# Attention scores from stacked rounded halves on the whole array, in a fused attention and two expert layers kernel

## The chip, the cores and the metric

One core of a Trainium2 chip. The metric is the device time of one execution in microseconds; the median of three runs is compared.

## The reference

```python
scores = scale * np.matmul(q, k.transpose(0, 1, 3, 2))     # B, H, S, D = 4, 8, 576, 64; fp32
scores = np.where(causal, -1e9, scores); a = softmax(scores)
local = np.matmul(a, v)
mem_out = einsum(phi(q), M_prev) / (einsum(phi(q), z_prev) + 1e-6)
x = g * mem_out + (1 - g) * local                          # g = sigmoid(beta), by head
h = x @ w_in;  x = (h * sigmoid(h)) @ w_out                # 2304 x 512 -> 2048 -> 512
g = x @ w_gate; out = (g * sigmoid(g) * (x @ w_val)) @ w_out   # 512 -> 1536 -> 512
```

The weights are float64; the rest is fp32.

## The kernel before, in words

Attention works on pairs of heads: the two 64-deep heads of a pair lie on partitions 0 to 63 and 64 to 127. The 576 query rows fall into blocks of 128 (blocks 0 to 3) and a last one of 64, and into two parts: the first 256 rows, and the other 320. There are three phases. Phase A is the first part of batch 0 (four pairs), phase B the second part of batch 0 (four pairs), phase F all rows of batches 1 to 3 (twelve pairs).

For a pair, `transposed` brings q and k into columns by TensorE (PE) transposes, and ScalarE (ACT) moves them out of PSUM as `Q` and `K` (in A and B `K` is the kept tile `kT`). `pa` makes phi(q). `s_blk(i)` computes the scores of block i, `w = 128 (i + 1)` keys wide, for both heads (line 394): a fp32 matmul of 64 rows each, with the query block as the stationary operand and the keys moving. VectorE (DVE) adds the mask and takes the row minimum (line 399; the sign of the scale is turned), ACT takes the exponential (line 403). `s_blk4` does the last 64 rows of both heads in one matmul on 128 rows. `norm` inverts the sums and GpSimd (POOL) scales the rows (line 436). `T_A` and `T_B` transpose the weights on PE, `AV` multiplies with v, and `put_x` splits the result into two rounded parts, `xh` and `xl`.

The two expert layers take every matrix product as three matmuls of fp32r, a rounded form of fp32: rounded by rounded, remainder by rounded, rounded by remainder. `s1` in `moe1` is the first product of the first layer (line 757, tile `h`), followed by tanh on ACT, a product on DVE (line 765), the rounding on ACT (`gh`) and the remainder on POOL (`gl`); line 801 is the second product (tile `y`). Lines 894 and 922 are those of the second layer. Weights are decoded from float64 by three DVE instructions (`decode`, lines 627 to 629) between a step on ACT and the rounding, and kept in DRAM as `wd` for later batches.

The order is made in two steps. The strings `opA`, `opB` and `opF` list a pair's steps, and each `+` ahead of a name moves it one slot on; the next pair begins 1, 7 or 8 slots later. `attn_slot` writes out one slot's steps; the loop at the end calls it at a rate set by the goals of the expert work of the first layer. Then the framework's scheduler reorders what was written by the times that it estimates; each engine executes its list in order. `att` gives the attention tiles their buffers: 4 in A, 2 in B, 2 in F.

Of the kernel before, what the change touches and what calls it, by code (L numbers as in the profile page):

```python
# [9 lines left out]
F32R = mybir.dt.float32r  # L10
# [7 lines left out]
P = 128  # L18
# [10 lines left out]
    T2=384,  # L29
# [22 lines left out]
    n0=8,  # L52
# [8 lines left out]
    ey=0,  # L61
    yr=['yx', 'y3'],
    n_rows=2,
    n_s4=dict(A=0, B=2, F=2),
    lb=3,
    bufsA={'*': 4},
    bufsB={'*': 2},
    bufsF={'*': 2},
    stepA=1,
    stepB=7,  # L70
    stepF=8,
    opA='q0 k0 ++pa s0 s1 ++m0 n0 ++TA ++V0',
    opB='q1 k1 ++pa lq ++s2 ++s3 ++m1 lb s4 ++++n1 +++T0 +T1 +T2 +T3 +T4 ++V1 lv',
    opF='q0 k0 +q1 k1 ++pa lq +s0 s1 ++s2 ++n0 s3 ++s4 m0 +m1 lb ++TA ++V0 n1 ++++T0 +T1 +T2 +T3 +T4 ++V1 lv',
    qev='a',
    kev='a',
    q4='p',
# [8 lines left out]
def kernel(  # L86
# [15 lines left out]
    nc = tc.nc  # L102
    B, H, S, D = q.shape
# [15 lines left out]
    def f(ap):  # L119
        return ap.bitcast(F32)  # L120
# [47 lines left out]
    cur = {}  # L168

    def att(shape, tag, bufs=1, dt=F32):  # L170
        return cur["pool"].tile(shape, dt, tag=tag, name=tag, bufs=cur["bufs"].get(tag, cur["bufs"].get("*", bufs)))

    def open_at(name):
        if "x" in cur:
# [13 lines left out]
    def cp(e, out, in_):  # L188
        if e == "a":
            nc.scalar.copy(out, in_)  # L190
        else:
            (nc.vector if e == "v" else nc.gpsimd).tensor_copy(out, in_)
# [7 lines left out]
    def tt(e):  # L200
        return nc.vector if e == "v" else nc.gpsimd
# [21 lines left out]
    def bd_of(u):  # L223
        b, p, _ = units[u]
        return bds[b % 2][:, p]
# [70 lines left out]
    def unit(u):  # L296
        b, p, sups = units[u]
        o = {}
        ph = "A" if sups == (0,) else "B" if sups == (1,) else "F"
        co = 0 if 0 in sups else SA  # L300
# [28 lines left out]
        def qT(sup):  # L329
            if "Q" not in o:  # L330
                o["Q"] = att([P, W], "Q", 2)
            d = slice(0, SA) if sup == 0 else slice(SA - co, S - co)
            transposed("q", sup, o["Q"][:, d], E("qev"), 1.0)
            if sup == 1:
                o["q4"] = q4s[u % 2]
                for hh in range(2):
                    r = slice(64 * hh, 64 * hh + 64)
                    cp(E("q4"), o["q4"][r, r], o["Q"][r, 512 - co:S - co])

        def kT(sup):  # L340
            if ph == "F":
                if "K" not in o:
                    o["K"] = att([P, S], "K", 2)
            else:
                if p not in keep:
                    keep[p] = kp.tile([P, S], F32, name=f"kT{p}")
                o["K"] = keep[p]
            d = slice(0, SA) if sup == 0 else slice(SA, S)
            transposed("k", sup, o["K"][:, d], E("kev"), QSCALE)

        def pa():
            e = att([P, W], "e", 2)
            qp = att([P, W], "qp", 2)
            nc.vector.tensor_scalar_min(e, o["Q"], 0.0)
            nc.scalar.activation(out=e, in_=e, func=ACTF.Exp)
            nc.vector.scalar_tensor_tensor(qp, o["Q"], 0.0, e, ALU.max, ALU.add)
            o["qp"] = qp

        def mm(sup):

            ps = ps_a.tile([P, 512], F32, tag="a", name="psm")
            for i, c in enumerate(BLK[sup]):
                x = P * c - co if c < 4 else S - P - co
                nc.tensor.matmul(ps[:, 130 * i:130 * i + 130], o["qp"][:, x:x + P], bd_of(u), start=True, stop=True)  # L364
            nb = len(BLK[sup])
            pv = ps[:, 0:130 * nb].rearrange("p (c n) -> p c n", c=nb)
            n = att([P, nb, 2], f"n{sup}", 2)
            nc.vector.tensor_scalar_add(n, pv[:, :, 128:130], 1.0e-6)
            nc.vector.reciprocal(n, n)
            nc.vector.tensor_mul(n, n, g_bc[:, hs2].unsqueeze(1).to_broadcast([P, nb, 2]))  # L370
            if sup == 1:
                nc.vector.memset(n[0:64, 2], 0.0)
            mr = att([P, nb, 2, D], f"mr{sup}", 2)
            nc.vector.tensor_mul(
                mr, pv[:, :, 0:128].rearrange("p c (h d) -> p c h d", h=2),
                n.unsqueeze(3).to_broadcast([P, nb, 2, D]),
            )
            o["mr", sup] = mr

        def new_small(sup):  # L380
            if ("mn", sup) in o:
                return
            o["mn", sup] = att([P, 8], f"mn{sup}", 2)
            o["sm", sup] = att([P, 8], f"sm{sup}", 2)

        def s_blk(i):
            sup = 0 if i < 2 else 1
            new_small(sup)
            w = P * (i + 1)
            pss = [ps_a.tile([P, 512], F32, tag="a", name="pss") for _ in range(2)]  # L390
            for hh in range(2):
                r = slice(64 * hh, 64 * hh + 64)
                x = P * i - co
                nc.tensor.matmul(pss[hh][:, :w], o["Q"][r, x:x + P], o["K"][r, 0:w], start=True, stop=True)  # L394
            for hh in range(2):
                col = (i % 2) * 2 + hh
                a = att([P, w], f"s{hh}{i}", 1)
                mn = o["mn", sup][:, col:col + 1]
                nc.vector.tensor_tensor_reduce(  # L399
                    out=a, in0=pss[hh][:, :w], in1=mask[:, 512 - w:512], op0=ALU.add, op1=ALU.min,  # L400
                    scale=1.0, scalar=3.0e38, accum_out=mn,
                )
                nc.scalar.activation(  # L403
                    out=a, in_=a, func=ACTF.Exp, scale=-1.0, bias=mn, accum_out=o["sm", sup][:, col:col + 1]
                )
                o["a", hh, i] = a
# [131 lines left out]
        def nxt_bd():  # L538
            if ph != "A" and p == NP - 1 and b + 2 < B:
                load_bd(b + 2, nc.sync)  # L540

        ops = {
            "q0": (qT, 0), "q1": (qT, 1), "k0": (kT, 0), "k1": (kT, 1), "pa": (pa,), "m0": (mm, 0), "m1": (mm, 1),
            "lq": (nxt_load, "qk"), "lv": (nxt_load, "v"), "lb": (nxt_bd,), "n0": (norm, 0), "n1": (norm, 1),
            "s4": (s_blk4,), "TA": (T_A,), "V0": (AV, 0), "V1": (AV, 1),
        }
# [2 lines left out]
        for i in range(4):  # L549
            ops["s%d" % i] = (s_blk, i)  # L550
# [3 lines left out]
        for nm in names:  # L554
            for d in DEPS.get(nm, "").split():
                assert d not in at_ or at_[d] < at_[nm], (d, nm)
# [12 lines left out]
        return CFG["step" + ph], [run(st) for st in stages]  # L569

    DEPS = dict(
        pa="q0 q1", s0="q0 k0", s1="q0 k0", s2="q1 k0 k1", s3="q1 k0 k1", s4="q1 k0 k1", lq="q0 q1 k0 k1",
        m0="pa", m1="pa", lb="m0 m1", n0="s0 s1", n1="s2 s3 s4", TA="n0", V0="TA m0", V1="T4 m1", lv="V0 V1",
        T0="n1", T1="T0", T2="T1", T3="T2", T4="T3",
# [5 lines left out]
    for u, key in enumerate(units):  # L580
        step, stages = unit(u)
        if u == NP:
            stages.insert(0, lambda: open_at("atB"))
            at_slot = max(slots) + 1
        if u == 2 * NP:
            stages.insert(0, open_F)
            at_slot = max(slots) + 1
        for i, st in enumerate(stages):
            slots.setdefault(at_slot + i, []).append(st)
        for sup in key[2]:  # L590
            ready[key[0], sup] = at_slot + len(stages)
        at_slot += step
# [235 lines left out]
    T2 = CFG["T2"]  # L828
# [103 lines left out]
    if True:  # L932
# [8 lines left out]
        for sg in segs:  # L941
            r = ready[sg["b"], sg["blk"][0] // SA]
# [5 lines left out]
        for kind, val in items:  # L948
# [7 lines left out]
            else:  # L956
                cost += val
                while goals and goals[0][0] <= cost:
                    c0, s0 = goals.pop(0)
                if goals:  # L960
                    x = (cost - c0) / (goals[0][0] - c0)
# [60 lines left out]
```

## Time and profile before

| | before |
|---|---|
| three runs, us | 1153.06, 1154.47, 1152.6 |
| median, us | 1153.06 |
| profiled execution: own time / span, us | 1154.19 / 1152.4 |
| granted TensorE clock, mean | 0.988 |
| busy: PE, DVE, ACT, POOL, us | 1120.4, 538.3, 440.4, 432.1 |
| DMA | 126.01 MB, mean 109 GB/s |

The span is that of the engines' instructions; the execution's own time holds 1.8 us more. A PE record's end is modelled and overlaps the next record, so what a matmul costs in a row of others is read from the distance of two starts.

### The profile page before, as it was taken

What the parts mean: (1) busy time and instruction counts of PE and PEld (TensorE: products, weight loads), DVE (VectorE), ACT (ScalarE), POOL (GpSimd) and SP (SyncE); (2) the same over time, 40 slices, a digit from 0 to 9 for tenths busy, and PEclk for the clock granted to TensorE, in tenths of its full rate; (3) what the DMA queues carried; (4) which work ended last, traced back from release to release, by engine and by line L of the source; (5) the groups of instructions that cost most, each with busy time, mean ns of one, the idle gap of its engine ahead of it and who ended that gap; (6) DMA issues with size and microseconds to landing.
All of it is one profiled execution on the core that took longest, in us unless ns stands there. A gap on an engine that the chain in (4) does not pass through costs nothing.

```text
span 1152.4 us, 18609 instructions
## 1 busy us (share of the span) xinstructions
PE 1120.4 (97%) x7016; PEld 1000.2 (87%) x7016; DVE 538.3 (47%) x1321; ACT 440.4 (38%) x1072; POOL 432.1 (37%) x480
## 2 busy tenths in 40 slices
PE   6899999999999999999989999989999999999998
PEld 4576877789989889989888999879999999999997
DVE  6996777785345442254397237852121211211211
ACT  6754766663443443343354214432121121211211
POOL 4575575564323323233275235552131311311311
PEclk8989999999999999999999999999999999999999
DMA  9975755462434413433178533420010000100000
GB/s 230 284 216 168 238 176 169 152 183 73 132 122 144 144 35 107 131 120 121 53 236 274 179 104 98 147 82 28 1 55 1 22 34 1 47 10 1 28 1 28
DMA packets 126634, 126.01 MB, mean 109 GB/s; under 512 B 72528, under 2 KB 108368, under 8 KB 126544
## 3 DMA queue, kind: packets, MB, share of 16 engines
q1 hardware_dynamic: 124368, 124.42, 34.7%
q8 instruction: 55, 0.90, 0.3%
q10 hardware_dynamic: 2176, 0.40, 0.2%
q14 instruction: 35, 0.29, 0.1%
HBM read 98.58 MB, written 26.21 MB: 108 GB/s over the span
## 4 chain that ended last, share of the span: by engine, by line
PE 82%; DVE 9%; ACT 3%; POOL 2%; issue 2%; DMA 1%; ACTq 0%; SPq 0%; POOLq 0%; DVEq 0%
PE g L894 23%; PE y L801 16%; PE h L757 16%; PE po L922 11%; PE pss L394 5%; PE U L527 4%; PE pst L317 3%; DVE raw L628 3%; DVE raw L629 2%; DVE raw L627 1%; PE psm L364 1%; ACT raw L626 1%; PE pss L422 1%; POOL wlo L669 1%; PE psq L317 1%
## 5 line engine op out<-in xcount | busy, mean ns | idle before, releaser
L767 POOL TENSOR_TENSOR gl<-th,gh 128x256 fp32r<-128x256 f32 (+1 forms) x128 | 108.6, 851 | 214.2 <-ACT gh L190 106.8
L909 POOL TENSOR_TENSOR pl<-sg,ph 128x384 fp32r<-128x384 f32 x71 | 74.3, 1046 | 300.6 <-ACT ph L907 300.6
L757 PE MATMUL h<-xh,w 128*128 128x320 f32 (+1 forms) x1024 | 170.3, 304 | 3.5 <-ACT w L190 1.2
L801 PE MATMUL y<-gh,w 128*128 128x320 f32 (+1 forms) x1024 | 167.7, 303 | 4.4 <-DVE th L765 4.4
L903 DVE SCALAR_TENSOR_TENSOR sg<-sg,g 128x384 f32<-128x384 f32 x72 | 39.7, 553 | 257.8 <-ACT sg L902 257.8
L757 PEld LDWEIGHTS h<-xh,w 128*128 128x128 f32 x1024 | 144.5, 190 | 18.0 <-issue 7.9
L801 PEld LDWEIGHTS y<-gh,w 128*128 128x128 f32 x1024 | 144.2, 190 | 17.5 <-issue 6.2
L436 POOL TENSOR_TENSOR s<-s,r 128x128 f32<-128x128 f32 (+4 forms) x144 | 115.3, 833 | 79.0 <-DVE r L453 41.1
L902 ACT ACTIVATE sg<-g 128x384 f32<-128x384 f32 x72 | 35.3, 491 | 190.2 <-PE g L894 190.2
L765 DVE SCALAR_TENSOR_TENSOR th<-th,h 128x256 f32<-128x256 f32 (+1 forms) x128 | 57.3, 449 | 98.5 <-ACT th L764 98.3
L894 PE MATMUL g<-yh,wlo 128*128 128x384 f32 x456 | 99.3, 337 | 1.5 <-POOL wlo L669 1.5
L894 PE MATMUL g<-yh,whi 128*128 128x384 f32 x456 | 98.8, 337 | 1.1 <-ACT whi L190 0.9
L894 PE MATMUL g<-yl,whi 128*128 128x384 f32 x456 | 99.4, 337 | 0.0
L801 PE MATMUL y<-gl,w 128*128 128x320 f32 (+1 forms) x512 | 92.9, 300 | 0.7 <-POOL gl L767 0.5
L757 PE MATMUL h<-xl,w 128*128 128x320 f32 (+1 forms) x512 | 92.9, 300 | 0.0
L190 ACT CAST gh<-th 128x256 fp32r<-128x256 f32 (+1 forms) x128 | 55.4, 432 | 93.7 <-DVE th L765 47.5
L907 ACT CAST ph<-sg 128x384 fp32r<-128x384 f32 x72 | 36.9, 513 | 138.1 <-DVE sg L904 138.0
L403 ACT ACTIVATE s<-s,mn 128x128 f32<-128x128 f32 (+3 forms) x128 | 71.3, 558 | 45.6 <-DVE mn L399 44.6
L894 PEld LDWEIGHTS g<-yh,whi 128*128 128x128 f32 x456 | 81.7, 188 | 7.0 <-ACT whi L190 1.3
L894 PEld LDWEIGHTS g<-yh,wlo 128*128 128x128 f32 x456 | 81.2, 188 | 1.9 <-POOL wlo L669 1.8
L894 PEld LDWEIGHTS g<-yl,whi 128*128 128x128 f32 x456 | 81.5, 189 | 0.0
L757 PEld LDWEIGHTS h<-xl,w 128*128 128x128 f32 x512 | 76.4, 191 | 4.5 <-issue 4.0
(110 smaller groups left out, 1950.5 us busy)
## 6 DMA issues: line engine op xcount, KB each, us to landing
w<-wd SPq DMA_DIRECT2D x80, 512.0 KB, 3.9
wd<-w SPq DMA_DIRECT2D x32, 512.0 KB, 4.0
raw<-in_moe_w_out_dram SPq DMA_DIRECT2D x28, 512.0 KB, 4.1
raw<-in_moe_w_in_dram SPq DMA_DIRECT2D x16, 512.0 KB, 5.0
raw<-in_moe_w_gate_dram SPq DMA_DIRECT2D x12, 512.0 KB, 3.6
raw<-in_moe_w_val_dram SPq DMA_DIRECT2D x12, 512.0 KB, 3.7
y<-yd SPq DMA_DIRECT2D x24, 192.0 KB, 2.5
out_dram<-ot SPq DMA_DIRECT2D x18, 256.0 KB, 2.1
```

The source lines that it names most:

```text
L190: nc.scalar.copy(out, in_)
L317: nc.tensor.matmul(dst, src, ident[0:n, 0:n], start=start, stop=True, is_transpose=True, skip_group_check=True)
L394: nc.tensor.matmul(pss[hh][:, :w], o["Q"][r, x:x + P], o["K"][r, 0:w], start=True, stop=True)
L403: nc.scalar.activation(out=a, in_=a, func=ACTF.Exp, scale=-1.0, bias=mn, accum_out=o["sm", sup][:, col:col + 1])
L436: nc.gpsimd.tensor_mul(a, a, r.to_broadcast([P, w]))
L757: nc.tensor.matmul(ps[:, :nt], w[:, kk, :], x[:, kk, :nt], start=(m == 0), stop=(m == 3 * KD - 1))
L765: nc.vector.scalar_tensor_tensor(th[:, :nt], th[:, :nt], 1.0, ps[:, :nt], ALU.add, ALU.mult)
L767: tt(CFG["gl" if n >= CFG["n0"] else "gl0"]).tensor_sub(gl[:, :nt], th[:, :nt], f(gh[:, :nt]))
L801: nc.tensor.matmul(ps[:, :nt], w[:, c], g[:, :nt], start=(m == 0), stop=(m == last))
L894: nc.tensor.matmul(ps[:, :T2], w[:, kk, :], y[kk], start=(m == 0), stop=(m == 3 * KD - 1))
L909: tt("v" if end else CFG["pl"]).tensor_sub(pl, sg, f(ph))
L922: nc.tensor.matmul(po[t], a[:, c], w, start=(j == 0 and n == 0), stop=(j == F2 - 1 and n == 2))
```

## The change

For blocks 0 to 3 in phase F and blocks 2 and 3 in phase B, a new step `st` (`stack`) builds three tiles in SBUF. `S` holds, for each head, the rounded q on the head's own 64 partitions and the remainder of q on the other 64. `Kh` holds the rounded k of the head on both halves, `Kl` the remainder of k on both halves. A block's scores are then two fp32r matmuls on all 128 rows that add up in PSUM: `S` against `Kh` and `S` against `Kl`. The roundings and copies are ACT's (two of q, four of k), one subtraction for each half of `S` and one half of `Kl` are DVE's, the other half of `Kl` POOL's. Phase A and the last 64 rows keep the old form.

The attention tiles of F get one buffer instead of two (also one `s4` tile); tiles of up to 8 columns get two in every phase, where A had four. The lists `opB` and `opF` are written anew: the last stage of a pair in F is 15 slots behind its first (25 before), in B 23 (21 before), and `lb`, the loads of M and z for the batch after the next, moves to the pair's end.

```diff
-    n_s4=dict(A=0, B=2, F=2),
+    n_s4=dict(A=0, B=2, F=1),
...
-    bufsF={'*': 2},
+    bufsF={'*': 1},
...
-    opB='q1 k1 ++pa lq ++s2 ++s3 ++m1 lb s4 ++++n1 +++T0 +T1 +T2 +T3 +T4 ++V1 lv',
-    opF='q0 k0 +q1 k1 ++pa lq +s0 s1 ++s2 ++n0 s3 ++s4 m0 +m1 lb ++TA ++V0 n1 ++++T0 +T1 +T2 +T3 +T4 ++V1 lv',
+    opB='q1 k1 ++pa lq st ++++s2 ++s3 ++m1 s4 ++++n1 +++T0 +T1 +T2 +T3 +T4 ++V1 lv lb',
+    opF='q0 k0 +q1 k1 ++pa lq st ++s0 s1 +s2 +s3 n0 +m0 m1 s4 +TA n1 +V0 ++T0 T1 +T2 T3 +T4 +V1 lv lb',
+    qh='a',
+    kh='aaaa',
+    kl='p',
...
     def att(shape, tag, bufs=1, dt=F32):
-        return cur["pool"].tile(shape, dt, tag=tag, name=tag, bufs=cur["bufs"].get(tag, cur["bufs"].get("*", bufs)))
+        return cur["pool"].tile(shape, dt, tag=tag, name=tag, bufs=cur["bufs"].get(tag, 2 if shape[-1] <= 8 else cur["bufs"].get("*", bufs)))
...
+        def stack():
+
+            nqs = 512 - co
+            S2 = att([P, 2, nqs], "S", 1, F32R)
+            KH, KL = (att([P, 2, 512], "K" + x, 1, F32R) for x in "hl")
+            Q, K = o["Q"][:, 0:nqs], o["K"][:, 0:512]
+            own_ = [slice(64 * hh, 64 * hh + 64) for hh in range(2)]
+            for hh in range(2):
+                r, x = own_[hh], own_[1 - hh]
+                cp(E("qh"), S2[r, hh], Q[r])
+                cp(E("kh")[hh], KH[r, hh], K[r])
+                nc.vector.tensor_sub(S2[x, hh], Q[r], f(S2[r, hh]))
+                cp(E("kh")[2 + hh], KH[x, hh], K[r])
+                tt(E("kl")).tensor_sub(KL[r, hh], K[r], f(KH[r, hh]))
+                nc.vector.tensor_sub(KL[x, hh], K[r], f(KH[r, hh]))
+            o["S"], o["KH"], o["KL"] = S2, KH, KL
...
+            x = P * i - co
             for hh in range(2):
-                r = slice(64 * hh, 64 * hh + 64)
-                x = P * i - co
-                nc.tensor.matmul(pss[hh][:, :w], o["Q"][r, x:x + P], o["K"][r, 0:w], start=True, stop=True)
+                if "S" in o:
+                    for n, part in enumerate(("KH", "KL")):
+                        nc.tensor.matmul(
+                            pss[hh][:, :w], o["S"][:, hh, x:x + P], o[part][:, hh, 0:w], start=(n == 0), stop=(n == 1)
+                        )
+                else:
+                    r = slice(64 * hh, 64 * hh + 64)
+                    nc.tensor.matmul(pss[hh][:, :w], o["Q"][r, x:x + P], o["K"][r, 0:w], start=True, stop=True)
```

Three places in the engines' lists. PE, third pair of batch 1, blocks 2 and 3 (`pss` are the scores, `h` and `y` the expert layer's two products, `pst` the transposes of the softmax rows, `U` the products with v), before:

```order
L394 MATMUL pss<-K,Q 128x384
L801 MATMUL y<-gl,w 128x320 x3
L394 MATMUL pss<-K,Q 128x384
L801 MATMUL y<-gh,w 128x320
L317 MATMUL pst<-ident,s_1449 128x128 x4
...
L394 MATMUL pss<-K,Q 128x512
L801 MATMUL y<-gh,w 128x320 x2
L394 MATMUL pss<-K,Q 128x512
```

and in the changed kernel:

```order
L415 MATMUL pss<-Kh,S 128x384
L415 MATMUL pss<-Kl,S 128x384
L828 MATMUL y<-gh,w 128x256 x3
L828 MATMUL y<-gl,w 128x256 x2
L415 MATMUL pss<-Kh,S 128x384
L415 MATMUL pss<-Kl,S 128x384
...
L415 MATMUL pss<-Kh,S 128x512
L415 MATMUL pss<-Kl,S 128x512
L415 MATMUL pss<-Kh,S 128x512
L415 MATMUL pss<-Kl,S 128x512
```

Before, the heads of a block stand apart, with expert matmuls between them; now each head's two matmuls follow each other, and whether the heads stand apart changes nothing in the rows used.

DVE, the first pair of phase B, before (`raw` is a weight being decoded):

```order
L628 SCALAR_TENSOR_TENSOR raw<-raw_317,raw 128x512
L354 TENSOR_SCALAR e<-Q 128x320
L629 SCALAR_TENSOR_TENSOR raw<-raw_317,raw 128x512
L356 SCALAR_TENSOR_TENSOR qp<-Q,e 128x320
L627 TENSOR_SCALAR raw<-raw 128x512
L628 SCALAR_TENSOR_TENSOR raw<-raw_373,raw 128x512
```

and in the changed kernel:

```order
L655 SCALAR_TENSOR_TENSOR raw<-raw_317,raw 128x512
L357 TENSOR_SCALAR e<-Q 128x320
L376 TENSOR_TENSOR Kl<-kT_157,Kh 64x512
L656 SCALAR_TENSOR_TENSOR raw<-raw_317,raw 128x512
L376 TENSOR_TENSOR Kl<-kT_157,Kh 64x512
L373 TENSOR_TENSOR S<-Q,S 64x256 x2
L359 SCALAR_TENSOR_TENSOR qp<-Q,e 128x320
L654 TENSOR_SCALAR raw<-raw 128x512
```

The four subtractions stand between the steps that decode the weights. ACT, the same pair in the changed kernel, where the four `Kh` and two `S` casts are new:

```order
L199 ACTIVATE Q<-psq 128x320
L193 CAST Kh<-kT_157 64x512 x4
L193 CAST S<-Q 64x256 x2
L358 ACTIVATE e<-e 128x320
L653 ACTIVATE raw<-raw_373 128x512
L193 CAST w<-raw 128x512
L791 ACTIVATE th<-h 128x256 x2
```

The six casts stand ahead of a weight's rounding and of the expert layer's first tanh.

## Rows read from the trace of the kernel before

**Rows 1.** Busy time of each engine by stretch.
```profile
core 0: us, PE busy (x) PEld busy (x) DVE busy (x) ACT busy (x) POOL busy (x), PEclk, DMA share, GB/s
119.00:546.00 427.00, 427.00 (x3036) 370.64 (x3035) 233.41 (x713) 210.83 (x565) 180.70 (x229) 1.00 0.44 137
30.00:119.00 89.00, 81.73 (x519) 61.25 (x520) 71.97 (x178) 51.63 (x128) 52.86 (x55) 0.92 0.72 218
```
**Rows 2.** The chain of waits from 119 to 546 us: shares by line.
```profile
by line: PE h L757 32.3%; PE y L801 31.6%; PE pss L394 11.1%; PE U L527 7.4%; PE pst L317 7.1%; PE psm L364 3.1%; PE pss L422 2.8%; PE psq L317 1.9%; PE psk L317 1.4%; PE U L317 1.3%
```
**Rows 3.** The chain of waits from 30 to 119 us (the answer ends there).
```profile
by line: PE h L757 8.6%; DVE raw L628 8.2%; issue 7.9%; PE y L801 7.7%; DVE raw L629 7.4%; PE U L527 7.3%; POOL s L436 7.2%; DVE s L399 5.4%; PE pss L394 4.3%; PE pst L317 3.6%; DVE tb L192 3.4%; ACT raw L626 3.4%; DVE raw L627 2.9%; DVE s 
```
**Rows 4.** Timeline of PE, lone heads: start, us, engine, line, operation, count.
```profile
83.75 0.28 PE L757 MATMUL h<-xl,w 128*128 128x256 f32 x1
83.97 0.91 PE L394 MATMUL pss<-kT,Q 64*128 64x384 f32 x2
84.80 0.63 PE L757 MATMUL h<-xl,w 128*128 128x256 f32 x3
85.27 0.99 PE L757 MATMUL h<-xh,w 128*128 128x256 f32 x7
...
133.88 0.48 PE L394 MATMUL pss<-K,Q 64*128 64x128 f32 x2
134.29 1.44 PE L801 MATMUL y<-gh,w 128*128 128x320 f32 x8
...
143.85 0.91 PE L394 MATMUL pss<-K,Q 64*128 64x384 f32 x2
144.69 1.14 PE L757 MATMUL h<-xh,w 128*128 128x320 f32 x6
...
146.71 1.12 PE L394 MATMUL pss<-K,Q 64*128 64x512 f32 x2
147.76 0.86 PE L527 MATMUL U<-ta,v_t 128*64 128x256 f32 x6
```
**Rows 5.** Timeline of PE, both heads next to each other.
```profile
329.08 0.92 PE L394 MATMUL pss<-K,Q 64*128 64x384 f32 x4
329.92 1.21 PE L801 MATMUL y<-gh,w 128*128 128x256 f32 x8
```
**Rows 6.** Timeline of PE, expert matmuls of 256, 384 and 512 columns.
```profile
663.79 0.64 PE L757 MATMUL h<-xl,w 128*128 128x256 f32 x4
664.27 1.12 PE L757 MATMUL h<-xh,w 128*128 128x256 f32 x8
...
796.75 0.86 PE L894 MATMUL g<-yl,whi 128*128 128x384 f32 x4
797.45 0.39 PE L922 MATMUL po<-whi,ph 128*128 128x512 f32 x1
797.68 0.39 PE L922 MATMUL po<-wlo,ph 128*128 128x512 f32 x1
```
**Rows 7.** ACT groups, 119 to 546 and 30 to 119 us: count, busy us, mean ns.
```profile
L190 ACT CAST w<-raw 128x512 fp32r<-128x512 f32 x16 | 9.8, 614 | 3.5 <-PE y L801 1.7 <-DVE raw L629 1.6
...
L190 ACT CAST gh<-th 128x256 fp32r<-128x256 f32 x8 | 3.2, 405 | 5.4 <-DVE th L765 5.4
```
**Rows 8.** A POOL group, 119 to 546 us.
```profile
L669 POOL TENSOR_TENSOR w<-raw,w 128x512 fp32r<-128x512 f32 x16 | 22.2, 1388 | 15.0 <-ACT w L190 12.8 <-issue 2.2
```
**Rows 9.** DVE line 628: min/median/max; groups of 119 to 546, 30 to 119 us.
```profile
L628 DVE SCALAR_TENSOR_TENSOR raw<-raw,raw x68: 674/693/1814, 15.0 to 764.4; 128x512 int32<-128x512 int32 x68
...
L628 DVE SCALAR_TENSOR_TENSOR raw<-raw,raw 128x512 int32<-128x512 int32 x16 | 12.7, 796 | 0.1
...
L628 DVE SCALAR_TENSOR_TENSOR raw<-raw,raw 128x512 int32<-128x512 int32 x14 | 14.3, 1024 | 0.2
```
**Rows 10.** A DVE group from 30 to 119 us.
```profile
L292 DVE TENSOR_TENSOR xl<-U,xh 128x256 fp32r<-128x256 f32 x3 | 1.2, 410 | 0.0
```
**Rows 11.** An ACT group of the whole span: the exponentials of block 3.
```profile
L403 ACT ACTIVATE s<-s,mn 128x512 f32<-128x512 f32 x32 | 23.0, 720 | 14.1 <-DVE mn L399 13.9
```

More of the change, by code (lines that the diff above doesn't have):

```diff
@@ L542, in unit @@
         ops = {
-            "q0": (qT, 0), "q1": (qT, 1), "k0": (kT, 0), "k1": (kT, 1), "pa": (pa,), "m0": (mm, 0), "m1": (mm, 1),
+            "q0": (qT, 0), "q1": (qT, 1), "k0": (kT, 0), "k1": (kT, 1), "pa": (pa,), "st": (stack,), "m0": (mm, 0), "m1": (mm, 1),
             "lq": (nxt_load, "qk"), "lv": (nxt_load, "v"), "lb": (nxt_bd,), "n0": (norm, 0), "n1": (norm, 1),
@@ L571 @@
     DEPS = dict(
+        st="q0 q1 k0 k1",
         pa="q0 q1", s0="q0 k0", s1="q0 k0", s2="q1 k0 k1", s3="q1 k0 k1", s4="q1 k0 k1", lq="q0 q1 k0 k1",
```

## The prediction

> **What bounds the kernel now.** I read first the busy times of the engines by stretch, since an average over the program hides the stages, then the chain of waits of each stretch, and last the timeline of the engine that the chain names [rows 1 to 4]. From 119 to 546 us, where pairs of heads of batches 1 to 3 are interleaved with the first expert layer, TensorE (PE) is busy for all of its 427.00 us [rows 1] and the chain of that stretch [rows 2] holds nothing but PE lines: there a microsecond less on PE is a microsecond less in the end, as long as nothing else comes last. From 30 to 119 us (second query blocks of batch 0, weights decoded for the first time) PE is busy for 81.73 of 89 us at a granted clock of 0.92, VectorE (DVE) for 71.97, and the chain [rows 3] changes hands: its visible PE lines (not all are printed) sum to 31.5%, DVE to 27.3%, POOL to 7.2%, ACT to 3.4%, "issue" to 7.9%. Behind 546 us come no scores; the change can only shift that part.
>
> Line 394, the scores that the change rewrites, is 11.1% of the first chain, 0.111 x 427 = 47.4 us, and 4.3% of the second, 3.8 us.
>
> **What a score block costs on PE now.** The timeline shows each head's matmul as two records, on 64 of the 128 rows. A 384-wide block of one head, with expert matmuls before and after it, takes PE from 83.97 to 84.80, 0.83 us, and another one 0.84 from 143.85; a 512-wide one takes 1.05, a 128-wide one 0.41 [rows 4]. Where both heads stand next to each other (four records) the two 384-wide ones together also take 0.84 us, from 329.08 to 329.92 [rows 5]: they run side by side. So what counts is the number of stretches, not of matmuls. Around each there is a toll: the one 256-wide matmul at 83.75 holds PE for 0.22 us instead of 0.12, and three behind the scores take 0.47 instead of 0.36 [rows 4, 6], together 0.20. I count 60 stretches between 119 and 526 us: 60 x 0.20 = 12 us, which the chain books to the neighbours. Sum for batches 1 to 3: 47.4 + 12 = 59.4 us.
>
> The Trainium skill (TensorEngine Tiling (Array Packing), section Theoretical Speedup) promises up to 2x from two row tiles where the contraction is 64 deep, which speaks against giving the tiles up. The trace agrees for adjacent heads [rows 5]; a lone head gets nothing of it [rows 4]. By the rule alone the old scores would cost 42 us instead of 59.4 (rival 4).
>
> **What takes its place.** Each head's block becomes two one-pass matmuls over all 128 rows (stacked q against the rounded k, then against its remainder). Rows 6 price that kind by the distance of starts: 256 wide 0.48/4 = 0.12 us, 384 wide 0.70/4 = 0.175, 512 wide 0.23. A 128-wide one is not in the trace: below it cannot cost nothing, above stands the pass of a lone 128-wide score, 0.41/2 = 0.205 [rows 4]; I take 0.12, the row of the same kind next to it. A pair: 4 x (0.12 + 0.12 + 0.175 + 0.23) = 2.58 us; twelve pairs 30.9 us, and no toll, since the neighbours use the whole array too. **Gain on PE: 59.4 - 30.9 = 28.5 us**, with 0.205 for the narrow blocks 24.4.
>
> **The stack step** is new in 16 pairs: six casts on ACT, four subtractions on DVE, two on POOL, 64 partitions each. A cast of 512 costs 0.61 us, of 256 0.41 [rows 7]; a subtraction on POOL 1.39 [rows 8]. On DVE a 512-long operation with two SBUF inputs takes 0.674 at the least and 1.814 at the most, on average 0.80 in the long stretch and 1.02 in the early one [rows 9]. That spread on one shape is a wait inside the instruction. The Trainium skill (GPSIMD Engine Reference, Key points) says that GpSimd shares its SBUF interfaces with VectorE and contends with DVE instructions that have two SBUF inputs, as all four subtractions have; the trace agrees in the spread. At the undisturbed median of 0.69 the step would cost a late pair 2.8 us of DVE, at the mean 3.2; I take the mean.
>
> From 119 us on that is 12 x 4 x 0.80 = 38 us more on DVE (233 to 271 of 398.5 us, 68%), 12 x 6 x 0.61 = 44 on ACT (211 to 255, 64%), 12 x 2 x 1.39 = 33 on POOL (181 to 214, 54%) [rows 1]. Idle time there hides it; without that cover, every microsecond that the step holds up an expert matmul comes back. In the order, the stack inputs stand several microseconds of expert matmuls ahead of their use. I charge 2 us in all for new waits.
>
> **Batch 0's second blocks, 30 to 119 us.** PE: by the order 11 stretches become 32 one-pass matmuls, 6 x 0.84 + 5 x 1.05 + 9 x 0.2 (where blocks follow each other the toll is paid once) = 12.1 us against 16 x (0.175 + 0.23) = 6.5, a gain of 5.6 if all of it ended last. DVE: 4 x (2 x 0.41 + 2 x 1.02) = 11 us more [rows 9, 10], ACT 4 x (4 x 0.61 + 2 x 0.41) = 13, POOL 8 x 1.39 = 11, the last two ahead of the weight splits that PE waits for. I scale each by its engine's visible share of the chain divided by 0.773, which the visible lines sum to: DVE 11 x 0.35 = 3.9, POOL 11 x 0.09 = 1.0, ACT 13 x 0.04 = 0.5, PE -5.6 x 0.41 = -2.3. **Net +3 us.** Bounds: -6 if PE sets it all; +14 if DVE goes on at its 81% share (11/0.81).
>
> **Other edits.** One buffer per attention tile costs nothing by itself as long as the shorter plan holds: a pair's list now spans 15 slots instead of 25 and the next pair starts 8 later, so each tile's last reader is placed ahead of its next writer. Where it does not hold, the writer waits on DVE or ACT, with the work of rival 2 behind it. The loads of M and z move to the end of their pair, on SP's queue behind a few row and weight loads that are needed sooner; their own next use is a batch later: nothing. The row loads keep their slot. The first query blocks of batch 0 keep the old form and, on PE, their old order.
>
> **Sum:** -28.5 + 3 + 2 = -23.5 us. The profiled execution took 1154.19 us, 1.13 above the median of the runs (1153.06), so 1130.7 for such an execution and **1130 us** against the median.
>
> **Rivals.**
> 1. DVE sets the pace up to 270 us. It is the fullest engine but PE in the early stretch, and the four pairs of batch 1 bring their step while weights are still decoded; a subtraction that waits behind POOL at 1.8 us delays the weights behind it. Then batch 1's four pairs gain nothing (-9.5 of the 28.5 gone) and the early stretch pays 14: -28.5 + 9.5 + 14 = -5, **1148 us**. For it: DVE's share of the chain, and its spread on one shape [rows 3, 9]. Against it: from 119 us on PE waits for nothing [rows 1].
> 2. Slower: the casts come as bursts on ACT, which takes its instructions in order. Six of 0.61 are 3.7 us per pair, put in front of the tanh and rounding steps that free the expert layer's three PSUM buffers and feed its second matmul. If all of it lands on PE: 12 x 3.7 = 44, -23.5 + 44 = +21, **1174 us**; it decides from 2.0 us per pair on. Against it: the two exponentials of a pair's block 3 alone already are 2 x 0.72 = 1.4 us in a row on ACT [rows 11], and PE had no idle time there.
> 3. All of PE's gain arrives, early stretch included, with no new wait: -28.5 - 6 = -34.5, **1119 us**. Against it: DVE's share of the early chain [rows 3].
> 4. In the old form both heads stand side by side in every block, and there is less to gain: with 0.41, 0.63 (between its neighbours), 0.84 and 1.05 for the four blocks and three tolls 12 x (2.93 + 0.6) = 42.4, less 30.9 = 11.5 gained, with the +5 of above -6.5, **1147 us**. Against it: the score line's share of the chain, and the lone heads [rows 2, 4]. This is the time by the tiling page of the Trainium skill (TensorEngine Tiling (Array Packing)).
>
> **How the numbers follow.** Forecast 0.68, rival 1 0.16, rival 2 0.08, rival 3 0.06, rival 4 0.02. The likeliest case with its bounds runs from 1120 (early stretch -6) to 1142 (narrow blocks 0.205, early stretch +11); the range reaches to rivals 3 and 1: **1116 to 1149 us**, which leaves out rival 2 and tails. About 0.2% (2.3 us) is what a measurement of this kernel can tell from no change. Faster: the forecast, rival 3, three quarters of 1 and half of 4, 0.87; slower: rival 2 and a rest, 0.09; same 0.04.
>
> **What would show it.** Right: the score lines fall to about 31 us of starts between 119 us and the last pair, 384- and 512-wide ones 0.17 and 0.23 apart with no longer step at either end; PE still without idle time after the first pairs; the early stretch at or a few microseconds above its 89 us; the last attention output some 25 us earlier; the stretch behind it as long as before. Wrong: PE waits for ACT's rounding or for the stacks in each pair (rival 2), DVE above 95% and PE idle up to 270 us (rival 1), or 128-wide matmuls more than 0.2 apart.

## The result, and the profile after

The changed kernel takes 1170.75 us (median of four, 1167.59 to 1171.83) against 1153.74 for the kernel before, run beside it: a ratio of 1.0144 [1.0121, 1.0166]. It is slower by 17 us, outside the predicted range and on the other side of no change.

Busy time of each engine over the whole span, from the page of the changed kernel:

```profile
PE 1103.5 (95%) x7016; PEld 1016.6 (87%) x7016; DVE 614.3 (53%) x1384; ACT 492.7 (42%) x1168; POOL 495.9 (43%) x512
```

PE is busy 16.9 us less than the 1120.4 before, and yet the span is 13.4 us longer (1165.8 against 1152.4). So PE has less to do, and idles more than it gained. DVE has 76 us more to do, POOL 64, ACT 52.

Busy time by stretch, changed kernel (rows 1 have the columns: after the length of the stretch PE, PEld, DVE, ACT, POOL with their counts, then the granted clock):

```profile
30.00:119.00 89.00, 68.11 (x428) 55.54 (x429) 81.73 (x181) 59.82 (x141) 63.18 (x60) 0.87 0.64 199
119.00:200.00 81.00, 73.27 (x509) 67.38 (x509) 70.47 (x151) 54.55 (x135) 53.17 (x52) 0.94 0.61 192
200.00:270.00 70.00, 61.95 (x436) 54.47 (x435) 64.45 (x155) 46.18 (x119) 45.36 (x46) 0.93 0.53 163
270.00:400.00 130.00, 129.37 (x979) 122.32 (x978) 71.88 (x196) 68.06 (x176) 59.00 (x70) 1.00 0.41 124
400.00:546.00 146.00, 145.65 (x1089) 137.08 (x1088) 76.33 (x219) 71.96 (x184) 59.76 (x71) 1.00 0.36 113
```

The same view of the kernel before, in two stretches that rows 1 do not show apart:

```profile
119.00:200.00 81.00, 81.00 (x498) 62.30 (x496) 63.22 (x190) 54.15 (x147) 50.88 (x60) 1.00 0.62 197
200.00:270.00 70.00, 70.00 (x491) 57.36 (x492) 51.44 (x154) 39.73 (x103) 38.07 (x44) 1.00 0.56 164
```

From 30 to 119 us PE was idle for 7.3 us before and is for 20.9 now; from 119 to 270 it was never idle and now is for 15.8. DVE is at 92% in the first (81.73 of 89), at 87% and 92% in the two parts of the second. From 270 to 546 us PE idles for 1 us in all. Over the whole span its idle time (span less busy time) rose from 32.0 to 62.3 us.

The granted clock fell with it, from 0.92 to 0.87 and from 1.00 to 0.94 and 0.93. The mean over the span is 0.978 instead of 0.988: 0.022 x 1165.8 = 25.6 us lost at the lower level against 0.012 x 1152.4 = 13.8, an estimate that takes PE as busy while the clock is low. The change of the span is 30.3 us more idle time less 16.9 us of busy time, +13.4. By the estimate those 16.9 hide about 12 us that matmuls lost at the lower clock, so that the scores saved about 29.

What PE waited for, changed kernel, from 30 to 119 us and then from 119 to 270 (us in all, times, longest):

```profile
PE pst L320 <- DVE mn L454: 5.2, 1, 5.2
PE pss L415 <- DVE S L373: 4.5, 3, 2.7
PE pst L320 <- POOL s L462: 2.2, 4, 0.9
PE pss L415 <- DVE mr L394: 2.2, 1, 2.2
```
```profile
PE pss L415 <- DVE xl L295: 6.2, 2, 5.3
PE pst L320 <- POOL s L462: 4.2, 3, 2.6
PE h L784 <- DVE yp L833: 1.8, 1, 1.8
```

Only some of these waits end with the new tiles (`S`); most end with old work of DVE and POOL (`mn`, the row minimum; `xl`; the scaled rows `s`) that now comes late. One such wait in the timeline of PE, and what follows it:

```profile
148.90 1.42 PE L828 MATMUL y<-gh,w 128*128 128x320 f32 x8
150.16 0.75 PE L828 MATMUL y<-gl,w 128*128 128x320 f32 x4
153.55 0.33 PE L320 MATMUL pst<-ident,s 128*128 128x128 f32 x1 [2.64 <-POOL s L462]
...
155.98 0.46 PE L415 MATMUL pss<-Kh,S 128*128 128x128 f32 x1
156.23 0.41 PE L415 MATMUL pss<-Kl,S 128*128 128x128 f32 x1
156.45 2.24 PE L784 MATMUL h<-xh,w 128*128 128x320 f32 x8
158.53 0.75 PE L784 MATMUL h<-xl,w 128*128 128x320 f32 x4
```

PE idles for 2.64 us, and soon behind that eight expert matmuls of 320 columns take 2.08 us from start to start; eight of the same width just before the wait took 1.26 (148.90 to 150.16). The granted clock is 1.00 from 148.9 to 151.0 us and 0.55 from 156.0 to 158.6: behind the idle stretch it has gone to the lower of its two levels (1.2 in place of 2.4 GHz) for most of them.

What kept DVE, in its timeline in the first pair of batch 1, and in its groups from 30 to 270 us (changed kernel; the last two lines are the decode, and behind them stand the same two before):

```profile
129.55 0.69 DVE L373 TENSOR_TENSOR S<-Q,S 64x512 fp32r<-64x512 f32 x1
130.27 3.43 DVE L376 TENSOR_TENSOR Kl<-K,Kh 64x512 fp32r<-64x512 f32 x2
133.73 0.29 DVE L425 CUSTOM_DVE_ANT_0 s<-pss,mask 128x128 f32<-128x128 f32 x1
```
```profile
L376 DVE TENSOR_TENSOR Kl<-K,Kh 64x512 fp32r<-64x512 f32 x10 | 13.5, 1350 | 0.3
...
L373 DVE TENSOR_TENSOR S<-Q,S 64x512 fp32r<-64x512 f32 x10 | 9.3, 935 | 0.6 <-ACT S L193 0.3
...
L655 DVE SCALAR_TENSOR_TENSOR raw<-raw,raw 128x512 int32<-128x512 int32 x30 | 31.0, 1035 | 0.3
L656 DVE SCALAR_TENSOR_TENSOR raw<-raw,raw 128x512 int32<-128x512 int32 x31 | 28.6, 922 | 0.3
```
```profile
L628 DVE SCALAR_TENSOR_TENSOR raw<-raw,raw 128x512 int32<-128x512 int32 x30 | 27.1, 903 | 0.3
L629 DVE SCALAR_TENSOR_TENSOR raw<-raw,raw 128x512 int32<-128x512 int32 x31 | 25.4, 818 | 0.1
```

Two subtractions hold DVE for 3.43 us, 1.7 each, where the one of `S` ahead of them takes 0.69, while POOL does the other half of the same remainder. On the mean one of `Kl` costs 1.35 us in these pairs (0.98 in batch 0's). The decode's two instructions rose too, from 0.903 and 0.818 us to 1.035 and 0.922: 7 us over the stretch.

### The profile page after: what moved, and what is told of

Read it like the earlier page. It is cut to its first block, busy times and chain, and to the rows that moved or that the text cites. A ratio compares the mean times of both kernels' runs of the same rounds, so it can differ in the third digit from the quotient of the medians.

```text
span 1165.8 us, 18836 instructions
## 1 busy us (share of the span) xinstructions
PE 1103.5 (95%) x7016; PEld 1016.6 (87%) x7016; DVE 614.3 (53%) x1384; ACT 492.7 (42%) x1168; POOL 495.9 (43%) x512
## 5 line engine op out<-in xcount | busy, mean ns | idle before, releaser
L794 POOL TENSOR_TENSOR gl<-th,gh 128x256 fp32r<-128x256 f32 (+1 forms) x128 | 112.1, 879 | 170.4 <-ACT gh L193 97.8
L828 PE MATMUL y<-gh,w 128*128 128x320 f32 (+1 forms) x1024 | 173.0, 305 | 4.4 <-DVE th L792 3.9
L462 POOL TENSOR_TENSOR s<-s,r 128x128 f32<-128x128 f32 (+4 forms) x144 | 124.6, 895 | 93.7 <-DVE r L479 49.9
L784 PEld LDWEIGHTS h<-xh,w 128*128 128x128 f32 x1024 | 148.9, 194 | 9.1 <-DVE yp L833 2.1
L828 PE MATMUL y<-gl,w 128*128 128x320 f32 (+1 forms) x512 | 95.6, 301 | 0.0
L429 ACT ACTIVATE s<-s,mn 128x256 f32<-128x256 f32 (+3 forms) x128 | 71.3, 559 | 38.0 <-DVE mn L425 37.4
L828 PEld LDWEIGHTS y<-gl,w 128*128 128x128 f32 x512 | 77.4, 190 | 1.5 <-issue 1.0
```

What stands on the lines that cost most here:

```text
L429: nc.scalar.activation(out=a, in_=a, func=ACTF.Exp, scale=-1.0, bias=mn, accum_out=o["sm", sup][:, col:col + 1])
L462: nc.gpsimd.tensor_mul(a, a, r.to_broadcast([P, w]))
L784: nc.tensor.matmul(ps[:, :nt], w[:, kk, :], x[:, kk, :nt], start=(m == 0), stop=(m == 3 * KD - 1))
L794: tt(CFG["gl" if n >= CFG["n0"] else "gl0"]).tensor_sub(gl[:, :nt], th[:, :nt], f(gh[:, :nt]))
L828: nc.tensor.matmul(ps[:, :nt], w[:, c], g[:, :nt], start=(m == 0), stop=(m == last))
```

## The experiments

All runs stand against the kernel before on the same chip, which took 1152.7 to 1152.9 us. Theory 1: the stack step's own work delays the engines that PE waits for while weights are being decoded (30 to 270 us); its readings 1a and 1b differ in how far POOL's two subtractions are to blame. Theory 2: the rewritten lists and the single buffers cost the time. Theory 3: PE waits for the chain from cast to subtraction to scores, which holds it in order; the step's load by itself is nearly free.

**The lists and buffers alone.** The step builds nothing, so the old score form runs in the new lists.

```diff
         def stack():
 
+            if b < 4:
+                return
```

> The changed kernel without the stack step in any pair: old scores, new step lists, one buffer per tile. Theory 1 (the step's work on DVE, POOL and ACT between 30 and 270 us, where weights are decoded, makes PE wait; the lists and buffers are harmless): 1150 to 1160 us, PE without idle time from 119 us on. Theory 2 (the new lists and single buffers take the look-ahead away and cost some 40 us, of which the cheaper scores give 24 back): about 1190 us, PE idle between 30 and 270 us for some 37 us as in the changed kernel.

1156.32 us (1151.37 to 1158.91), ratio 1.0020 [1.0002, 1.0038]. Theory 2 explains about 2 of the 17 us (0.2 to 4.4 by the interval). From here on this kernel is the base from which the step is counted.

**The step from batch 2 on, and from batch 1 on.** The same edit with `b < 2` and with `b < 1`.

> Stack step only in the eight pairs of batches 2 and 3, old scores in batches 0 and 1. Theory 1: 8 x 2.4 = 19 us below the kernel without the step, 1132 to 1142 us, PE idle before 270 us as in the kernel before (about 17 us). Theory 2: 19 us below a kernel that loses 40, about 1172 us.

> Stack step in the twelve pairs of batches 1 to 3, old scores in batch 0. Theory 1: the 13.6 us more of PE idle time between 30 and 119 us go, those between 119 and 270 us (16 us) stay: 1145 to 1158 us. Theory 2: 1170 us as the changed kernel, or above it.

From batch 2: 1143.98 us, 0.9921 [0.9907, 0.9936]. From batch 1: 1156.91 us, 1.0041 [1.0027, 1.0054]. So the eight pairs of batches 2 and 3 give 12.3 us, 1.5 per pair (less than the expectation's 19, and the time lies 2 us above its range); the four of batch 1 take 13 back, and the four of batch 0 cost 14 more (1170.75 - 1156.91; 12 by the ratios). The change pays where the weights come ready from DRAM and costs where they are decoded. The stretches from 119 to 200 and 200 to 270 us of the kernel from batch 1 show the cost of batch 1 without batch 0:

```profile
119.00:200.00 81.00, 72.91 (x495) 66.34 (x496) 73.00 (x171) 56.26 (x142) 55.11 (x54) 0.94 0.63 198
200.00:270.00 70.00, 61.91 (x439) 55.58 (x438) 62.53 (x152) 45.43 (x112) 45.73 (x46) 0.93 0.49 147
```

**POOL's two subtractions moved to DVE.** `kl='v'` in place of `kl='p'`.

> All six subtractions of the step on DVE, none on POOL. If the wait inside DVE's two-input instructions behind POOL's own part of the step is what costs (theory 1a), DVE's subtractions fall from 1.1 to 1.25 us towards 0.7, six take about what four took (4.3 against 4.7 us a pair), and the time falls by 3 to 10 us, to 1160 to 1168. If DVE's plain load sets the pace (theory 1b), the time rises or stays: 1170 to 1182.

1168.36 us, 1.0132 [1.0117, 1.0147], 2.4 us under the changed kernel and by the intervals not to be told from it; it lies between the two forecasts. The subtractions of `Kl` on DVE fell to a mean of 0.97 to 1.02 us (512 long, batches 1 and 2, 30 to 270 us, from 1.35), but there are two more of them. The relief that 1a asks for is there in the single instruction and mostly lost to the added load, as 1b has it; neither placing is good.

**The step built, the old scores kept.** Everything is built, and nobody reads it. Three more runs keep one engine's part of it alone; in two of them a subtraction's operands are the same tile twice, since its rounded one is not made.

```diff
-                if "S" in o:
+                if "S" in o and CFG["qh"] == 'x':
```

> The whole stack step runs in all 16 pairs, but no matmul reads it: scores are the old ones. Compare with the kernel without the step (1156.3 us). Theory 1 (the step's load on DVE, POOL and ACT delays everything behind it): 1178 to 1192 us, above the changed kernel by the 10 to 15 us that the cheaper scores give late. Theory 3 (PE waits for the chain cast, subtraction, scores, which holds it in order): nothing waits for the tiles here, so 1156 to 1163 us.

DVE's four subtractions alone:

```diff
-                cp(E("qh"), S2[r, hh], Q[r])
-                cp(E("kh")[hh], KH[r, hh], K[r])
-                nc.vector.tensor_sub(S2[x, hh], Q[r], f(S2[r, hh]))
-                cp(E("kh")[2 + hh], KH[x, hh], K[r])
-                tt(E("kl")).tensor_sub(KL[r, hh], K[r], f(KH[r, hh]))
-                nc.vector.tensor_sub(KL[x, hh], K[r], f(KH[r, hh]))
+                nc.vector.tensor_sub(S2[x, hh], Q[r], Q[r])
+                nc.vector.tensor_sub(KL[x, hh], K[r], K[r])
```

> Only the four DVE subtractions of each step (of q and q, k and k; not read by anything), no casts, no POOL part, old scores. Theory 1 with DVE as the engine that decides: 60% or more of the rise of the run with the whole step: 1170 to 1182 us. If ACT or POOL decide: 1156 to 1163.

ACT's six casts alone (the three `cp` lines stay), and POOL's two subtractions alone (`nc.gpsimd.tensor_sub(KL[r, hh], K[r], K[r])` stays):

> Only the six ACT casts of each step, not read by anything, old scores. If the casts in front of tanh and rounding decide (rival 2 of the prediction): 1170 us and more. With DVE as the engine that decides: 1156 to 1164.

> Only the two POOL subtractions of each step, not read by anything, old scores. POOL is busy for 60% of 30 to 119 us. If only DVE's time counts: 1156 to 1160. If POOL's own queue or the waits that it puts into DVE's instructions count: 1160 to 1170.

| part of the step, unread | us | ratio | over the lists alone |
|---|---|---|---|
| all | 1202.46 | 1.0419 [1.0393, 1.0445] | 46.1 |
| DVE | 1179.18 | 1.0222 [1.0198, 1.0245] | 22.9 |
| ACT | 1157.95 | 1.0048 [1.0032, 1.0064] | 1.6 |
| POOL | 1160.79 | 1.0060 [1.0043, 1.0078] | 4.5 |

Two results stand on this table. Theory 3 falls as the main cause: the step costs 46 us where nothing reads it (more than the range expected), and the new scores, for which this kernel and the changed one differ, save 1202.46 - 1170.75 = 31.7, their waits included. (Such waits are there in the changed kernel, 4.5 us for `S` in the rows above and 2.5 for `Kl` in rows not shown.) And DVE's part is the dearest by far, though half of the whole and not the 60% expected; ACT's 96 casts cost almost nothing. The parts add up to 29.0, not 46.1; 17 us belong to the parts together. (The runs of the lists alone scatter by 7.5 us, so 1.6 is not to be told from nothing.) More than half of the step's cost is not idle time on PE. The same matmuls keep PE busy for 27 us longer (of 45 between the two profiled executions), at a mean granted clock of 0.970 against 0.990 in the lists alone, while its idle time rises from 33.9 to 52.2 us; the pages' lines for the lists alone and for the whole step:

```profile
PE 1121.6 (97%) x7016; PEld 1000.8 (87%) x7016; DVE 538.4 (47%) x1320; ACT 441.4 (38%) x1072; POOL 435.5 (38%) x480
```
```profile
PE 1148.2 (96%) x7016; PEld 1013.8 (84%) x7016; DVE 611.9 (51%) x1384; ACT 492.3 (41%) x1168; POOL 497.3 (41%) x512
```

Busy time by stretch, the lists alone first, then DVE's part alone:

```profile
30.00:119.00 89.00, 82.39 (x535) 61.48 (x531) 71.27 (x178) 52.38 (x131) 53.08 (x56) 0.96 0.75 226
119.00:270.00 151.00, 149.37 (x1017) 123.63 (x1016) 116.35 (x310) 87.83 (x233) 87.21 (x97) 1.00 0.57 179
```
```profile
30.00:119.00 89.00, 71.75 (x425) 50.47 (x421) 80.78 (x185) 48.30 (x119) 52.25 (x53) 0.90 0.69 213
119.00:270.00 151.00, 142.72 (x959) 117.01 (x957) 124.63 (x303) 83.09 (x221) 86.03 (x89) 0.97 0.56 173
```

DVE's subtractions alone take it from 80% to 91% in the first stretch; PE loses 10.6 us of busy time in it, and the granted clock falls from 0.96 to 0.90. In that kernel one 512-long subtraction of `Kl` takes 1.14 us and one of `S` 0.98 (30 to 270 us); in the one with the whole step 1.51 and 1.21. With the shorter ones that `kl='v'` gave, this says that a part of what the parts cost together is DVE held up by POOL's subtractions; where the rest of the 17 us comes from was not measured.

**The second halves of k by DMA.** The other head-half of `Kh` and of `Kl` is copied from the first, SBUF to SBUF; two of the four subtractions on DVE and two casts on ACT go.

```diff
-                cp(E("kh")[2 + hh], KH[x, hh], K[r])
+                nc.sync.dma_start(out=f(KH[x, hh]), in_=f(KH[r, hh]))
...
-                nc.vector.tensor_sub(KL[x, hh], K[r], f(KH[r, hh]))
+                nc.sync.dma_start(out=f(KL[x, hh]), in_=f(KL[r, hh]))
```

It was run in all 16 pairs, from batch 1 on and from batch 2 on (with the guard of above).

> In all 16 pairs, the second halves of the k tiles are copied inside SBUF by DMA: per pair DVE does two subtractions (of q) instead of four, ACT four casts instead of six, POOL its two. Theory 1: the step's 46 us fall by half of DVE's part and of the part that DVE and POOL put on each other, to 22 to 32 us: 1147 to 1158 us. If the DMAs' latency of some microseconds now gates the scores: above 1165 us.

> The same in batches 1 to 3 only. Theory 1: below e3 (1156.9) by 6 to 12 us, 1145 to 1151. If the DMA latency gates: 1157 or more.

> The same in batches 2 and 3 only, where PE hides the step already in e2 (1144.0): no difference, 1142 to 1146 us. If the DMA latency gates: 1147 or more.

All pairs: 1153.70 us, 1.0012 [1.0003, 1.0022], 17 us better than the change. From batch 1: 1144.86, 0.9926 [0.9905, 0.9948], 12 better than its counterpart. From batch 2: 1145.25, 0.9935 [0.9917, 0.9953], the same as its counterpart. Taking work off DVE (and two casts off ACT, which cost almost nothing above) pays in batches 0 and 1, where DVE is full, and gives nothing in batches 2 and 3, most of which lie behind 270 us, where it is not: theory 1, by its place. The copies run from batch 1, stretches as above:

```profile
119.00:200.00 81.00, 72.95 (x508) 68.20 (x507) 63.75 (x150) 51.74 (x128) 56.82 (x55) 0.96 0.76 230
200.00:270.00 70.00, 68.43 (x503) 61.28 (x503) 57.24 (x163) 43.90 (x119) 42.48 (x47) 1.00 0.55 160
```

DVE comes down from 73.00 and 62.53 to 63.75 and 57.24 us; PE has 6.5 us more of the second stretch, at full clock. In the first it has nothing more (72.95 against 72.91), though DVE was relieved of 9 us: PE now waits there for DVE's product behind the tanh (`th`, 3.6 us in two waits) and for the load of a decoded weight (2.5 us). So DVE's busy share does not by itself tell what PE gains.

**No subtraction on DVE at all, from batch 1.** As the last but one, and the remainder of q on POOL (`nc.gpsimd.tensor_sub` in place of `nc.vector.tensor_sub`).

> In batches 1 to 3, copies by DMA and the remainders of q on POOL too: DVE has no part in the step, POOL four subtractions, ACT four casts. Theory 1 with DVE as the engine that decides: below e10, 1130 to 1143 us. If POOL's queue takes DVE's place: as e10 or above, 1146 to 1156.

1153.98 us, 1.0023 [1.0007, 1.0040], 9 us worse than with that subtraction on DVE, in the place of the second forecast. DVE is busy for 107.6 of the 151 us from 119 to 270, against 121.0 in the kernel that it is compared with, and yet PE idles for 11.7 us there instead of 9.6, and for 2.9 from 270 to 546 us instead of none. What PE waited for on the new tiles, from 119 to 270 us and from 270 to 546:

```profile
PE pss L417 <- DMA Kl<-Kl: 1.7, 1, 1.7
PE pss L417 <- POOL S L375: 0.7, 2, 0.5
```
```profile
PE pss L417 <- DMA Kl<-Kl: 2.8, 3, 1.1
```

POOL's subtraction of `S` (1.47 us each from 30 to 270 us) stands ahead of that of `Kl`, whose copy the scores wait for; here theory 3's chain costs time. PE has no wait for a weight's split on POOL from 119 to 546 us. So it is not DVE's load alone that counts; where the rest of the 9 us comes from stays open.

Three kernels beat both the kernel before and the changed one: the step in batches 2 and 3 alone (1143.98 us, or 1145.25 with the DMA copies), and the DMA copies from batch 1 on (1144.86). They cannot be told apart. Two buffers beside the stack tiles were not tried, so it is not shown what the single buffers cost once the step is in place.

## Why the prediction was wrong

**The gain on PE was right.** Forecast 28.5 us for batches 1 to 3 and 5.6 at most for batch 0, 34.1 together; 31.7 by the unread step, waits for the tiles included. The one-pass prices hold, as the timeline of PE in the changed kernel shows, four 512-wide matmuls behind the product with v:

```profile
312.77 1.14 PE L553 MATMUL U<-tb,v_t 128*64 128x320 f32 x10
313.84 0.50 PE L415 MATMUL pss<-Kh,S 128*128 128x512 f32 x1
314.18 0.40 PE L415 MATMUL pss<-Kl,S 128*128 128x512 f32 x1
314.41 0.40 PE L415 MATMUL pss<-Kh,S 128*128 128x512 f32 x1
314.64 0.40 PE L415 MATMUL pss<-Kl,S 128*128 128x512 f32 x1
314.88 1.33 PE L784 MATMUL h<-xh,w 128*128 128x320 f32 x8
```

Starts lie 0.23 apart; a toll of 0.1 is left at the first, behind a matmul that uses 64 columns of the array. At full clock a 128-wide one takes 0.11, under the 0.12 taken and far from the bound of 0.205.

**Its spread over the pairs.** The forecast gave each of the twelve pairs 2.4 us. Busy time of line 394 before, by stretch, and then of the same old scores (line 422) in the kernel with the lists alone:

```profile
119.00:270.00 151.00, 31.43 (x96) 11.46 (x96) 1.00 0.59 182
270.00:546.00 276.00, 20.16 (x96) 7.70 (x96) 1.00 0.36 113
```
```profile
119.00:270.00 151.00, 22.46 (x80) 8.70 (x80) 1.00 0.57 179
270.00:600.00 330.00, 27.93 (x112) 10.57 (x112) 1.00 0.36 115
```

In the old order six pairs stand on each side of 270 us. The early ones cost more, since late pairs have their heads next to each other more often (22 stretches of scores against 38 early): with the tolls, by the distance of starts, 36.4 and 22.7 us. Less 6 x 2.58 each, 21 of the gain's 28 us lay ahead of 270 us. The new lists change that. By the timeline of PE five pairs stand ahead of 270 us, in 26 stretches, and seven behind, in 31; counted in the same way they cost 25.8 and 31.9 us, and 12.9 and 13.8 are left to gain, 2.6 and 2.0 per pair. So the even spread was near enough for the new lists, but by luck: the prediction read it from the old ones. Rival 4's rule (heads side by side leave less to gain) held for the late half of the old order.

**The step that failed is the price of the stack step**: "+3" for batch 0, nothing but "2 us in all for new waits" from 119 us on. It costs 46 us. Worked out by place, with these gains per pair: batch 0 had 5.6 to gain at most and lost 12 to 14, a cost of 18 to 20; batch 1 had 4 x 2.6 = 10 to gain and lost 13, a cost of 23; batches 2 and 3 had 2.6 + 7 x 2.0 = 16.6 and got 12.3, a cost of 4. The sum is 45 to 47, beside the 46 measured at once. (Both hold the same loss of 14.4 us against the lists alone; what agrees is the gain, 32 here and 31.7 there.) Three things in the working of that step were wrong:

1. The cover. "Idle time there hides it", from "233 to 271 of 398.5 us, 68%", is an average over two stages. From 119 to 200 us DVE was already at 78% before the change (63.22 of 81), and with the step at 87%; from 270 to 546 us it is at 54% even with the step. The prediction began by saying that an average hides the stages, and took one here.
2. The price. A subtraction was put at the mean of line 628 in the late stretch, 0.80 us, and at 1.02 in the early one; in batches 1 to 3 one of `S` took 1.09 and one of `Kl` 1.25, and the decode that it stands among got longer as well. In batch 0 the short ones of `S`, put at 0.41, took 0.90. DVE's 76 us more compare with 49 forecast, POOL's 64 with 44; ACT's 52 with 57 was right.
3. The scaling in batch 0. DVE's share of the chain, 0.35, was taken as the part of added DVE work that ends last. Work added to an engine that is busy for 81% of a stretch, on whose results PE waits in order, does not keep the old shares. The bound of +14, by DVE's busy share, is near the net loss of 12 to 14, but it counted no gain on PE, and the cost alone was 18 to 20: a part of that is luck.

And one price was missing: where PE waits, the clock that it gets falls, and by the estimate above some 12 us of the loss are matmuls at the lower level rather than idle time.

**The rivals.** Rival 1 had the place right and the mechanism in the main (DVE sets the pace to 270 us; PE idles there, as its sign says, though DVE stays at 87 to 92% and under the 95% that was named). It charged too little: batch 1's gain lost and 14 us in batch 0, where batch 1 also paid 13 on top of its lost gain. With that it would have been -5 + 13 = +8, and slower; with 12.3 gained in batches 2 and 3 in place of 19, and 2 for the lists, it is the +17. "From 119 us on PE waits for nothing", the argument against it, told of the old load only. Rival 2, the casts on ACT, came out nearest to the time by its number, 1174 us, for a wrong reason: the casts alone cost 1.6 us. **Other edits** at nothing: the lists and buffers cost 0.2 to 4.4 us by their interval, near the nothing that was put down.

## What to carry to other kernels

Put the gain and the cost of a change into the same stretches before adding them up: here somewhat over half of the gain and nearly all of the cost lay where the helpers were full, and doing the step in half of the pairs turned +17 us into -9. In this kernel an engine busy for 78 to 81% of a stage, on whose results another one waits in order, had no free time to hide the step in. Building the new operands without using them separates the price of the preparation from the gain of the use in one run.

## What was not expected of the hardware

- A copy of half a tile from SBUF to SBUF by DMA, 64 copies of 128 KB in all pairs, took 17 us off the changed kernel in place of engine copies and subtractions. Its two groups among the DMA issues of that run (KB each, median us from issue to landing):

```profile
Kh<-Kh SPq DMA_DIRECT2D x32, 128.0 KB, 3.3
Kl<-Kl SPq DMA_DIRECT2D x32, 128.0 KB, 2.9
```

  In batches 2 and 3, where nothing on DVE was to be gained, they changed nothing that can be told (0.9935 against 0.9921, intervals overlapping), so it is not shown that they are faster than the engines' copies, only that they pay where DVE is full.
- A two-input operation of DVE on one shape (64 x 512) took from 0.684 to 1.76 us in the changed kernel, with a median of 1.37 for `Kl<-K,Kh`; the spread that line 628 showed before [rows 9] is not its own: it came to the new instructions as well, and more so where POOL worked on the same tiles (0.97 to 1.02 us on the mean where POOL's part was moved away, 1.35 where not). The Trainium skill (GPSIMD Engine Reference, Key points) names the shared SBUF interface for such pairs of instructions; the runs agree in direction (1.51 us in the kernel with the whole step, 1.14 in the one with DVE's part alone).
- Casts on ACT of 64 partitions take as long as those of 128: 0.618 us (`Kh`) against 0.617 (`w`) for 512 columns, 30 to 270 us.
